# Polysketch attention and hash-routed experts on one core: q's features made with features on partitions

## Chip, core and metric

The kernel runs on one core of one Trainium2 chip. The metric is the time of one execution on the device in microseconds (us); lower is better. The time before is the median of three runs.

## The reference

```python
# q, k, v: (4, 4, 1088, 32) f32;  S1, S2: (8, 32) f64;  w1: (8, 128, 1024);  w2: (8, 1024, 128)
def phi(x):
    a = np.einsum('rd,bhsd->bhsr', S1, x)
    b = np.einsum('rd,bhsd->bhsr', S2, x)
    return np.einsum('bhsi,bhsj->bhsij', a, b).reshape(*x.shape[:-1], 64)
q_p, k_p = phi(q), phi(k)
kv = np.einsum('bhsf,bhsd->bhfd', k_p, v)
z = np.sum(k_p, axis=2)
num = np.einsum('bhsf,bhfd->bhsd', q_p, kv)
den = np.einsum('bhsf,bhf->bhs', q_p, z)[..., None] + 1e-06
x = (num / den).transpose(0, 2, 1, 3).reshape(4352, 128)

expert_idx = token_ids * 2654435761 % 8
for e in range(8):
    mask = expert_idx == e
    out[mask] = np.maximum(x[mask] @ w1[e], 0) @ w2[e]
```

Each row of q and k becomes 64 features, the products of 8 numbers from S1 with 8 numbers from S2. Everything after that is linear attention, and then one of eight experts for each token.

## The kernel before, in words

There are two stages: attention by batches (four of them, 0 to 3), and experts by groups of tokens. The order of the instructions of every engine is written out by hand: what stands in the source from top to bottom is what each engine gets, in its own queue and in that order. Tiles come from pools, and a pool with n buffers makes the n+1st tile wait until the first is read.

The attention of a batch of 1024 + 64 rows (the 64 are the "tail", kept in tiles of their own for all batches) goes so. `turned` and `turned_all` transpose k and q on TensorE, 128 rows by 128 columns at a time (four groups of 32 head columns), into one PSUM bank per half batch, and ScalarE copies them to `kT` and `qT`. `s_products` multiplies these as the stationary operand with `s_k`, the sketch laid out as a block diagonal of 128 rows by 64 columns. So the rows of the batch come out on partitions, and a and b of each of them lie along the free axis. ScalarE copies the a part (`first_copied`), and `features` multiplies a and b on VectorE to the 64 features of each row: `kp` for k, `f` for q, two instructions of 1024 columns each. `kv_products` accumulates kp against the values `va`, whose 33rd column of ones yields z. For q the 64 features must stand on partitions in the last product, so `q_turned` and `f_turned` transpose `f` again: 16 transposes a batch in four banks, each copied out to `fT` by ScalarE (by VectorE for every other one in the first and the last batch, `EVICT`). `x_products` multiplies fT with `m`, the kv product, in three PSUM tiles of at most three columns of rows each, ScalarE copies them to `xe`, `denominators` makes the reciprocals, and `x_main` (POOL, for batch 2 VectorE) and `x_rows` (DMA on SP's queue) write the rows to `x_rows` in DRAM.

The products of 64 columns run in two column halves of TensorE (`HALVES`, `tile_position=(0, 0)` or `(0, 64)`).

Between these stand, on VectorE and POOL above all, the steps that sort the tokens by expert (`route_...`). They end in `route_list`, 34 small matmuls, and `route_end`, which gives the index lists `get` and `put`.

In the expert stage `fetch_tile` gathers rows from DRAM by an indirect DMA on POOL's queue, `bring` and `bring_tile` transpose them on TensorE, `layer1` (L919) and `layer2` (L927) are the two products, `evict` takes layer 1 out of PSUM, and `scatter` writes the result. The last batch's x products stand in the first expert group, beside layer 1.

PSUM has eight banks: four in the pool `ps` (tag "b"), two in `ps_x` (tag "x") and two in `ps_o` (tag "o").

Of the kernel before, what the change touches and what calls it, by code (L numbers as in the profile page):

```python
# [30 lines left out]
def kernel(  # L31
# [12 lines left out]
    nc = tc.nc  # L44
# [37 lines left out]
    ps = ctx.enter_context(tc.tile_pool(name="ps", bufs=4, space=bass.MemoryType.PSUM))  # L82
    ps_x = ctx.enter_context(tc.tile_pool(name="ps_x", bufs=2, space=bass.MemoryType.PSUM))
    ps_o = ctx.enter_context(tc.tile_pool(name="ps_o", bufs=2, space=bass.MemoryType.PSUM))

    def bank(shape, name):
        return ps.tile(shape, F32, tag="b", name=name)

# [130 lines left out]
    def keep_busy(n, psum=None):  # L219

        if n == 0:
            return
        p = psum([P, 512], "idle") if psum else ps_o.tile([P, 512], F32, tag="o", name="idle")
        for _ in range(n):
            nc.tensor.matmul(p[:], warm[:].to_broadcast([P, P]), warm[:].to_broadcast([P, 512]), start=True, stop=True)

    keep_busy(WARM)
# [52 lines left out]
    s_k = const.tile([P, Q, 2, R], F32)  # L280

    def s_turned(psum):
        s_ps = psum([P, 2 * R], "s_ps")
        nc.tensor.transpose(s_ps[:], s_rep[:].rearrange("p t d -> p (t d)"), ident[:2 * R, :2 * R])
        nc.vector.tensor_tensor(s_k[:].rearrange("p t x r -> p t (x r)"), s_ps[:].unsqueeze(1).to_broadcast([P, Q, 2 * R]),
                                own_t[:].unsqueeze(2).to_broadcast([P, Q, 2 * R]), op=OP.mult)

# [32 lines left out]
    def route_counts():  # L320
        cnt = bank([P, 3, E], "cnt")
# [116 lines left out]
    def route_list():  # L438
        idx_ps = bank([P, 2, SE], "idx_ps")
# [23 lines left out]
    def x_bank(shape, name):  # L463
        return ps_x.tile(shape, F32, tag="x", name=name)

    def o_bank(shape, name):
        return ps_o.tile(shape, F32, tag="o", name=name)
# [4 lines left out]
    def turned(src, which):  # L472

        def half(g, heads=range(H)):
            p = bank([P, len(heads), P], "T_ps")
            for i, h in enumerate(heads):
                nc.tensor.transpose(p[:, i], src[:, h, g * Q:(g + 1) * Q].rearrange("p t d -> p (t d)"), ident[:])
            return p

        sT = work.tile([P, GQ, H, P], F32, tag=which, name=which, bufs=1)  # L480
        return sT, half

    def turned_all(src, which):
        sT, half = turned(src, which)
        for g in range(GQ):
            nc.scalar.copy(sT[:, g], half(g)[:])
        return sT
# [6 lines left out]
    def tail_products(sT):  # L494

        ab = bank([P, 2, TT, H, 2 * R], "abt_ps")
# [16 lines left out]
    def ab_bank(psum=o_bank):  # L513
        return psum([P, GQ, Q, H, 2 * R], "ab_ps")
# [58 lines left out]
    def f_turned(f, i):  # L573

        p = bank([P, 2, H // 2, P], "fT_ps")
        for t in range(2):
            for pr in range(H // 2):
                nc.tensor.transpose(p[:, t, pr], f[:, 2 * i + t, 2 * pr:2 * pr + 2].rearrange("p h i j -> p (h i j)"), ident[:])  # L578
        return p

    def q_turned(f, engs):

        fT = work.tile([P, T, H // 2, P], F32, tag="fT", name="fT", bufs=1)
        for i, eng in enumerate(engs):
            copy_of(eng)(fT[:, 2 * i:2 * i + 2], f_turned(f, i)[:])
        return fT

    def x_products(b, fT, m, psums=(x_bank, bank, x_bank)):

        for i, psum in enumerate(psums):  # L590
            lo = 3 * i
            n = min(3, T - lo)
            p = psum([P, n, H, DA], "x_ps")
            for t in range(n):
                for pr in range(H // 2):
                    for c, r in enumerate(HALVES):
                        nc.tensor.matmul(p[r, t, 2 * pr:2 * pr + 2].rearrange("p h d -> p (h d)"), fT[:, lo + t, pr, r],  # L597
# [4 lines left out]
    def x_tail_products(b, m, psum=x_bank):  # L602
# [113 lines left out]
    def bring(k, psum=x_bank):  # L716
# [32 lines left out]
    EVICT = (A, V, A, V)  # L749
    kT, _ = turned(k_t[0], "kT")  # L750

    def turned_head(src, sT, h):
        p = bank([P, GQ, P], "T_ps")
        for g in range(GQ):
            nc.tensor.transpose(p[:, g], src[:, h, g * Q:(g + 1) * Q].rearrange("p t d -> p (t d)"), ident[:])
        nc.scalar.copy(sT[:, :, h], p[:])

    for h in range(H):
        turned_head(k_t[0], kT, h)
        if h == 2:  # L760
            s_turned(x_bank)
    route_experts()
    ak, kp = first_of_ab(), feature_tile("kp")
    abk = [ab_bank(), ab_bank()]
# [5 lines left out]
    keep_busy(2, bank)  # L770
    qT, _ = turned(q_t[0], "qT")
    abq, aq, f = ab_bank(x_bank), first_of_ab(), feature_tile("f")
    for h in range(H + 1):
        if h < H:
            turned_head(q_t[0], qT, h)
        if h > 0:
            s_products(abq, qT, range(GQ), [h - 1])
    values(0, slice(0, H // 2), nc.scalar.copy)
    first_copied(aq, abq, range(GQ))
    values(0, slice(H // 2, H))  # L780
    kv = kv_products(0, kp, range(T), pairs=(0,))
    kv_products(0, kp, range(T), kv, (1,))
    nc.scalar.copy(cp[:], seq[:, :, C - 1])
    cnt = route_counts()
    features(f, aq, abq, range(GQ))
    route_places(cnt)
    route_order()
    kT = turned_all(k_t[1], "kT")
# [3 lines left out]
    def tail_f_turned():  # L792
        p = bank([P, TT, H // 2, P], "fTt_ps")
# [5 lines left out]
    for b in range(B - 1):  # L799
        last = b == B - 2  # L800
        if b > 1:
            kT = turned_all(k_t[b + 1], "kT")
        if b == 1:
            q_t.append(load_main(q, 3, "q", A.memzero))
        if last:
            qT = turned_all(q_t[b + 1], "qT")
        fT = q_turned(f, (A, A, A, A) if b > 0 else EVICT)
        if b == 0:
            route_bases(cnt)
            digits = route_ranks()  # L810
            tail_ps = bank([P, 2, TT, P], "tail_ps")
            tail_turned(k_tail, tail_ps, 0)
            tail_turned(q_tail, tail_ps, 1)
            tailT = work.tile([P, 2, TT, P], F32, tag="tailT", name="tailT", bufs=1)
            nc.scalar.copy(tailT[:], tail_ps[:])
            qT = turned_all(q_t[1], "qT")
            for u, va_tail in enumerate(va_tails):
                rows = tail_rows(u * TT)
                nc.gpsimd.tensor_copy(va_tail[rows, :, :, 0:D], v_tail[rows])
            tail_features(tail_products(tailT))  # L820
            route_parts(digits)
            route_order_end()
        elif not last:
            qT = turned_all(q_t[b + 1], "qT")
        if b == 1:
            v_t.append(load_main(v, 2, "v", A.memzero))
            route_in_tile()
        if last:
            idx = route_list()
            route_end(idx)  # L830
        if b > 0:
            kv = kv_products(b, kp, range(T + 1))
            m = kv_diagonal(b, kv)
        if b == 1:
            route_tiles_p()
        if last:
            load_expert(0, (2,), A.memzero)
        abq, aq, f = ab_bank(), first_of_ab(), feature_tile("f")
        s_products(abq, qT, range(GQ))
        first_copied(aq, abq, range(GQ))  # L840
        abk, ak, kp = ab_bank(), first_of_ab(), feature_tile("kp")
        s_products(abk, kT, range(GQ))
        first_copied(ak, abk, range(GQ))
        if b == 0:
            q_t.append(load_main(q, 2, "q", A.memzero))
            kT, half = turned(k_t[2], "kT")
            nc.scalar.copy(kT[:, 0], half(0)[:])
# [3 lines left out]
            nc.scalar.copy(kT[:, 1], half(1)[:])  # L851
        values(b + 1)
        if b == 1:
            v_t.append(load_main(v, 3, "v", A.memzero))
            load_expert(0, (1,))
            route_rows(0)
            route_tiles()
            route_rows(1)
            denominators(0)
            x_main_all(0)  # L860
            for g in range(GQ):
                x_rows(0, g)
            x_tail_rows(0)
        features(f, aq, abq, range(GQ))
        if b == 0:
            route_slots()
        x_products(b, fT, m)
        x_tail_products(b, m)
        if b == 0:
            k_t.append(load_main(k, 3, "k", A.memzero))  # L870
        if last:
            load_expert(1, (1,), A.memzero)
        if b == 0:
            features(kp, ak, abk, range(GQ))
        elif last:
            features(kp, ak, abk, range(GQ))
            denominators(b)
        else:
            denominators(b)
            features(kp, ak, abk, range(GQ))  # L880
        if 0 < b and not last:
            x_main_all(b)
        if b == 1:
            for g in range(GQ):
                x_rows(1, g)
            x_tail_rows(1)
        if last:
            for j in range(tiles_of(0)[1]):
                fetch_tile(0, j, True)

    e = B - 1
    fT = q_turned(f, EVICT)
# [4 lines left out]
    bring(0, o_bank)  # L897
    kv = kv_products(e, kp, range(T // 2, T + 1), kv)
# [6 lines left out]

    hots.release()
# [7 lines left out]
    def layer1(g, c, lo=0, hi=None):  # L914
# [3 lines left out]
        hp = bank([P, GL], "hp")  # L918
# [4 lines left out]
    def layer2(g, c, lo=0, hi=None):  # L923
        hi = hi or size_of(g)
        if c == 0:
            ops[g] = ps_o.tile([P, GL], F32, tag="o", name="op")
# [65 lines left out]
    def out_rows(i, n):  # L992
        tp = ps_x.tile([P, CT, P], F32, tag="x", name="tp")
# [51 lines left out]
    at(0, x3, x_products, e, fT, last_m)  # L1045
    at(0, x3, x_tail_products, e, last_m)
# [194 lines left out]
```

## Time and profile before

| | us |
|---|---|
| median of three runs | 180.3 (179.45 to 180.99) |
| profiled execution | 179.0 |
| its span | 177.2 |
| TensorE busy | 170.0 (96%) |
| VectorE busy | 95.8 (54%) |
| ScalarE busy | 67.7 (38%) |
| POOL busy | 93.4 (53%) |
| first matmul of layer 1 starts | 48.31 |

Engines in the profile: PE is TensorE's matmuls and PEld its weight loads, DVE is VectorE, ACT is ScalarE, POOL is GpSimd, SP issues most DMAs. The second part of the page cuts the span into 40 equal slices, 4.4 us each, and shows the busy share of each in tenths. In the timeline a line stands for a run of like instructions: its start, its length, the engine, the line of the source, the operation, output<-inputs, shape, and the number of records. TensorE is drawn as busy while a matmul is anywhere in its pipeline, so the starts tell more than the lengths.

### The profile page before, as it was taken

To read this page: it belongs to the slowest core of one execution; us is meant where nothing else is said; L and a number is where in the kernel's file an instruction comes from. 1 tells how busy PE (TensorE), PEld (TensorE's weight loads), DVE (VectorE), ACT (ScalarE), POOL (GpSimd) and SP (SyncE) were. 2 spreads that over 40 slices of the span, in tenths; PEclk is the share of its full clock that TensorE was granted. 3 is DMA by queue.
4 is the path that set the end of the run, shared out by engine and by line. 5 is a ranking of instruction groups with operands and counts; after the bars stand their busy time and mean duration, and the time that the engine had idled before them with its cause. 6 is when DMAs were issued, how large, how long until landed. Compare 5 with 4: busy or idle time off the path is not lost. (4 is left out here: it accounts for less than half of the span.)

```text
span 177.2 us, 4349 instructions
## 1 busy us (share of the span) xinstructions
PE 170.0 (96%) x1571; PEld 142.9 (81%) x1571; DVE 95.8 (54%) x309; ACT 67.7 (38%) x183; POOL 93.4 (53%) x134
## 2 busy tenths in 40 slices
PE   7899999999999999999999999999999999999980
PEld 3579899999886888888777778788788777778980
DVE  3688998996944333625535253535548543432330
ACT  3548686846452323133231422323232331320330
POOL 7313441774258366677756243773774760405752
PEclk9999999999999999999999999999999999999997
DMA  4897459485676869994983644484441522300100
GB/s 134 263 244 166 153 131 325 171 319 142 182 244 190 275 154 184 233 205 99 230 140 82 199 118 94 124 209 93 110 110 39 117 74 45 74 19 29 58 25 29
DMA packets 39382, 25.83 MB, mean 146 GB/s; under 512 B 20964, under 2 KB 35557, under 8 KB 39360
## 3 DMA queue, kind: packets, MB, share of 16 engines
q1 hardware_dynamic: 36944, 20.98, 45.4%
q0 software_dynamic: 2240, 4.53, 9.4%
q8 instruction: 13, 0.21, 0.5%
q14 instruction: 9, 0.07, 0.1%
q10 hardware_dynamic: 176, 0.04, 0.1%
HBM read 17.41 MB, written 4.52 MB: 124 GB/s over the span
## 5 line engine op out<-in xcount | busy, mean ns | idle before, releaser
L927 PE MATMUL op<-hT,w 128*128 128x256 f32 (+8 forms) x256 | 76.3, 389 | 0.0
L650 DVE TENSOR_SCALAR hT<-hp 128x256 f32<-128x256 f32 (+9 forms) x68 | 29.1, 428 | 59.1 <-PE hp L919 56.3
L927 PEld LDWEIGHTS op<-hT,w 128*128 128x128 f32 x256 | 47.5, 190 | 10.5
L930 POOL DMA_INDIRECT out_dram<-os,put x35 | 35.2, 1006 | 33.2 <-DVE os L988 16.3
L648 ACT ACTIVATE hT<-hp 128x256 f32<-128x256 f32 (+9 forms) x68 | 26.6, 391 | 63.2 <-PE hp L919 61.6
L642 POOL DMA_INDIRECT xg<-x_rows,idx x33 | 34.5, 1047 | 21.3 <-DVE idx L709 12.1
L919 PE MATMUL hp<-xT_late,w 128*128 128x320 f32 (+8 forms) x144 | 41.7, 385 | 0.0
L919 PE MATMUL hp<-xT,w 128*128 128x256 f32 x128 | 37.7, 381 | 0.0
L919 PEld LDWEIGHTS hp<-xT_late,w 128*128 128x128 f32 x144 | 25.3, 190 | 4.7
L919 PEld LDWEIGHTS hp<-xT,w 128*128 128x128 f32 x128 | 23.9, 191 | 5.5 <-ACT hT L648 0.4
L532 DVE TENSOR_TENSOR f<-first_of_ab,ab_ps 128x1024 f32<-128x1024 f32 x8 | 9.3, 1205 | 2.0 <-ACT first_of_ab L525 2.0
L532 DVE TENSOR_TENSOR kp<-first_of_ab,ab_ps 128x1024 f32<-128x1024 f32 x8 | 9.3, 1208 | 0.9 <-ACT first_of_ab L525 0.9
L561 PE MATMUL kv<-va,kp 128*64 128x33 f32 x256 | 8.4, 224 | 0.1
L561 PEld LDWEIGHTS kv<-va,kp 128*64 128x64 f32 x256 | 7.9, 138 | 0.8 <-issue 0.4
L597 PE MATMUL x_ps<-m,fT 128*64 128x66 f32 x256 | 8.3, 222 | 0.0
L552 POOL COPY va<-v 128x1024 f32<-128x1024 f32 (+1 forms) x4 | 3.7, 930 | 8.6 <-ACT v L117 4.3
L597 PEld LDWEIGHTS x_ps<-m,fT 128*64 128x64 f32 x256 | 7.8, 137 | 0.5 <-issue 0.5
L988 DVE COPY os<-turned 128x256 uint16<-128x256 uint16 (+1 forms) x26 | 7.3, 324 | 1.6 <-DMA xg<-x_rows,idx 1.0
L967 ACT COPY half<-op 128x256 uint16<-128x256 uint16 x16 | 5.2, 375 | 7.5 <-PE op L927 7.5
L578 PE MATMUL fT_ps<-ident,f 128*128 128x128 f32 x64 | 7.8, 274 | 0.0
L734 DVE COPY xh<-xg 128x256 uint16<-128x256 uint16 (+1 forms) x26 | 7.0, 313 | 1.2 <-DMA xg<-x_rows,idx 1.0
L578 PEld LDWEIGHTS fT_ps<-ident,f 128*128 128x128 f32 x64 | 7.0, 141 | 0.1
(199 smaller groups left out, 165.5 us busy)
## 6 DMA issues: line engine op xcount, KB each, us to landing
w<-in_moe_w_dram SPq DMA_DIRECT2D x20, 256.0 KB, 2.9
w<-in_moe_w_dram SPq DMA_DIRECT2D x6, 512.0 KB, 4.8
x_rows<-xs SPq DMA_DIRECT2D x8, 256.0 KB, 4.9
k<-in_k_dram SPq DMA_DIRECT2D x3, 512.0 KB, 6.8
q<-in_q_dram SPq DMA_DIRECT2D x3, 512.0 KB, 3.8
v<-in_v_dram SPq DMA_DIRECT2D x3, 512.0 KB
out_dram<-os,put POOLq DMA_INDIRECT x35, 2.5
xg<-x_rows,idx POOLq DMA_INDIRECT x33, 3.7
```

Of the source, the lines that this page charges most:

```text
L532: nc.vector.tensor_tensor(dst[:].rearrange("p t h i j -> p (t h) i j")[:, r], a[:, r].unsqueeze(3).to_broadcast(shape), rows_of_ab(ab)[:, ...
L561: nc.tensor.matmul(kv[h * R * R:(h + 1) * R * R, pr], f[:, 2 * pr + h].rearrange("p i j -> p (i j)"), v_[:, 2 * pr + h], start=(t == 0 and ...
L578: nc.tensor.transpose(p[:, t, pr], f[:, 2 * i + t, 2 * pr:2 * pr + 2].rearrange("p h i j -> p (h i j)"), ident[:])
L597: nc.tensor.matmul(p[r, t, 2 * pr:2 * pr + 2].rearrange("p h d -> p (h d)"), fT[:, lo + t, pr, r], m[:, pr].rearrange("p h d -> p (h d)"), ...
L642: nc.gpsimd.indirect_dma_start(out=dst, out_offset=None, in_=x_dram[0:rows], in_offset=bass.IndirectOffsetOnAxis(ap=idx, axis=0), bounds_c ...
L648: nc.scalar.activation(dst, src, AF.Relu if relu else AF.Copy)
L650: return nc.vector.tensor_scalar(dst, src, 0.0, None, op0=OP.max).ins
L734: nc.vector.tensor_copy(xh[:, x * w:(x + 1) * w], _half(xg3[k][:].rearrange("p a b -> p (a b)")[:, 0:w], x))
L919: nc.tensor.matmul(hp[:, 0:hi - lo], w1[:, g % E, c * P:(c + 1) * P], x_columns(first_of(g) + lo, first_of(g) + hi), start=True, stop=True)
L927: nc.tensor.matmul(ops[g][:, 0:hi - lo], w2[:, g % E, c], hTs[g][:, c, lo:hi], start=(c == 0), stop=(c == FC - 1))
L930: st_ = nc.gpsimd.indirect_dma_start(out=out[:], out_offset=bass.IndirectOffsetOnAxis(ap=idx, axis=0), in_=src, in_offset=None, bounds_che ...
L988: nc.vector.tensor_copy(_half(os[:].rearrange("p a b -> p (a b)"), x)[:, 0:n * DM], tts[x][:, 0:n].rearrange("p a b -> p (a b)"))
```

## The change

q's features are no longer made with rows on partitions and then transposed. Instead the sketch itself, each of its numbers repeated so that it has 64 columns for a and 64 for b (`s_q`), is the stationary operand, and `qT` is the moving one. The contraction is over the 32 columns of one head and one group of rows, so that a product takes 32 rows by 64 columns of TensorE, with 256 columns moving; `tile_position` names one of four row groups and one of two column halves. a and b come out with the 64 features on partitions; ScalarE copies a (`q_copied`), VectorE multiplies (`q_features`), and the result is `fT`. A batch is done in two pairs of heads, 16 products each. k's features are made as before.

```diff
+    one = ctx.enter_context(tc.tile_pool(name="one", bufs=1, space=bass.MemoryType.PSUM))
+    ps_q = tc.alloc_tile_pool(name="ps_q", bufs=2, space=bass.MemoryType.PSUM)
...
+    s_q = const.tile([P, 2, R, R], F32)
...
+        nc.vector.tensor_copy(s_q[:, 0], s_ps[:, 0:R].unsqueeze(2).to_broadcast([P, R, R]))
+        nc.vector.tensor_copy(s_q[:, 1], s_ps[:, R:2 * R].unsqueeze(1).to_broadcast([P, R, R]))
...
-    def f_turned(f, i):
-        p = bank([P, 2, H // 2, P], "fT_ps")
-        for t in range(2):
-            for pr in range(H // 2):
-                nc.tensor.transpose(p[:, t, pr], f[:, 2 * i + t, 2 * pr:2 * pr + 2].rearrange("p h i j -> p (h i j)"), ident[:])
-        return p
-    def q_turned(f, engs):
-        fT = work.tile([P, T, H // 2, P], F32, tag="fT", name="fT", bufs=1)
-        for i, eng in enumerate(engs):
-            copy_of(eng)(fT[:, 2 * i:2 * i + 2], f_turned(f, i)[:])
-        return fT
+    def q_products(qT, pr):
+        ab = [two_banks([P, 2, 2, GQ, P], "ab_q") for i in range(Q // 2)]
+        for c, cols in enumerate(HALVES):
+            for x in range(2):
+                for t in range(Q):
+                    rows = slice(t * D, (t + 1) * D)
+                    nc.tensor.matmul(ab[t // 2][cols, t % 2, x].rearrange("p g n -> p (g n)"),
+                                     s_q[rows, x].rearrange("p i j -> p (i j)"), qT[rows, :, 2 * pr + c],
+                                     start=True, stop=True, skip_group_check=True, tile_position=(rows.start, cols.start))
+        return ab
+    def q_copied(ab):
+        a = work.tile([P, 2, GQ, P], F32, tag="first_q", name="first_q", bufs=2)
+        nc.scalar.copy(a[:], ab[:, :, 0])
+        return a
+    def q_features(fT, pr, firsts, abs_):
+        fT[pr] = work.tile([P, GQ, Q, P], F32, tag="fT", name="fT", bufs=3)
+        for i, (a, ab) in enumerate(zip(firsts, abs_)):
+            nc.vector.tensor_tensor(fT[pr][:, :, 2 * i:2 * i + 2].rearrange("p g t n -> p t g n"), a[:], ab[:, :, 1], op=OP.mult)
```

In the attention stage PSUM is now two tiles of two banks each for q's products (`ps_q`, `two_banks`) and four single banks, each a tag of its own with one buffer: t and a (transposes, k's products) and x and y (kv, x products, tails). When the stage ends, `ps_q` is given up and the pool `ps` of four banks takes its place; the experts use t and a by turns where `ps_o` was, x and y by turns where `ps_x` was.

The order inside a batch is new. For batches 1 and 2 it reads (leaving out the steps of routing, the loads and the rows):

```python
kv = kv_products(b, kp, range(Q), own([P, H // 2, DA], "kv"))      # first half of the rows
k_half(1, t_bank if b == 1 else a_bank)()                          # k of the next batch
abq = q_products(qT, 1)
aq = [q_copied(ab) for ab in abq]
q_features(fT, 1, aq, abq)
s_products(abk, kT, range(GQ))
first_copied(ak, abk, range(GQ))
q_pair(0)()                                                        # q of the next batch
kv_products(b, kp, range(Q, T + 1), kv)
m = kv_diagonal(b, kv)
features(kp, ak, abk, range(GQ))
abq = q_products(qT, 0)                                            # of the next batch
aq = [q_copied(ab) for ab in abq]
q_features(next_fT, 0, aq, abq)
x_products(b, fT, m, range(2), (other, own))
q_pair(1)()
x_tail_products(b, m, other)
x_products(b, fT, m, range(2, 3), (0, 0, own))
denominators(b)
```

Routing moves with it: `route_list` of batch 2 stands behind q's second pair and k's products, and `route_slots` stands ahead of kp's first half in batch 0. In the last batch q's second pair stands between `bring(0)` and the second part of the kv products, just ahead of the experts.

## Prediction

> **What bounds the kernel now.** I read the page's busy table and slices first, then TensorE's waits, then the timeline of TensorE, and last the single start times of its matmul records, because a busy TensorE is not yet a full one.
>
> ```profile
> PE 170.0 (96%) x1571; PEld 142.9 (81%) x1571; DVE 95.8 (54%) x309; ACT 67.7 (38%) x183; POOL 93.4 (53%) x134
> PE   7899999999999999999999999999999999999980
> DVE  3688998996944333625535253535548543432330
> ```
>
> TensorE is the bound from about 10 us on. VectorE is close to it only in slices 3 to 11 (9 to 49 us), the attention stage that the change rewrites. The expert stage behind it (48 to 171 us) keeps its instructions, so what counts is by how much its first matmul, L919 at 48.31, moves.
>
> ```profile
> PE idle L225 <- POOL warm L180: 1.0, 1, 1.0
> PE s_ps L284 <- DVE s_rep L275: 0.4, 1, 0.4
> PE xp L726 <- DMA xg<-x_rows,idx: 0.3, 1, 0.3
> PE ab_ps L510 <- ACT qT L756: 0.2, 1, 0.2
> ```
>
> These are all of TensorE's waits: 1.9 us, none of them between 10 and 48 us. No eviction or feature product delays it there, so a shorter path on another engine gains nothing, and only TensorE's own work counts. One batch (b=1) in the timeline:
>
> ```profile
> 23.74 1.97 PE L578 MATMUL fT_ps<-ident,f 128*128 128x128 f32 x16
> 25.54 1.04 PE L477 MATMUL T_ps<-ident,q 128*128 128x128 f32 x8
> 26.51 2.06 PE L561 MATMUL kv<-va,kp 128*64 128x33 f32 x64
> 28.40 0.41 PE L561 MATMUL kv<-va_tail,f_tail 128*64 128x33 f32 x8
> 28.63 1.13 PE L510 MATMUL ab_ps<-s_k,qT 128*64 128x64 f32 x32
> 29.59 1.10 PE L510 MATMUL ab_ps<-s_k,kT 128*64 128x64 f32 x32
> 30.53 2.05 PE L597 MATMUL x_ps<-m,fT 128*64 128x66 f32 x64
> 32.40 0.40 PE L606 MATMUL x_ps<-m,fT_tail 128*64 128x66 f32 x4
> ```
>
> Columns: start, length, operation, records. Every matmul of this f32 data that is not a transpose leaves two records. The batch takes 8.99 us (23.74 to 32.73). Three prices come from the single starts. A transpose costs 109 ns. A 64-column record costs 29.2 ns where the two column halves alternate (L597, L510), but 58 ns where all sit on one half (L606): two halves really run at once. There the records start in pairs 7 ns apart from the very first, so a half is not held back by the other half's second record. Third, a change of tiling: the first 64-column record starts 203 ns after the last transpose (109 would be normal) and the second pair comes 20 to 48 ns late; back again it is 150 ns instead of 58, and the next gap 165 instead of 109. That is about 0.15 us for each change.
>
> **What the Trainium skill says.** TensorEngine Tiling (Array Packing), Key Properties: different tiles load and multiply in parallel, but changing the tiling mode drains the engine. The trace agrees with both (29 against 58 ns; 0.15 us). TensorE: Matmul & The Clock Gate, Part 3 (Measured speedup vs the span model): four row tiles of 32 gave 3.07 times, 16 row and column tiles 10.6 times, while matmuls start strictly in program order; the pairs 7 ns apart do not look like strict order if a matmul's two records stand together. No row tile is in the trace of before. TensorEngine Tiling, Gotcha 1: row tiles must write different PSUM banks; this is why the change needs two tiles of two banks.
>
> **The change, part by part.**
>
> Removed on TensorE: 64 transposes of f (L578), 64 x 109 = 7.0 us, and q's half of L510, 128 records x 29.2 = 3.7 us. Sum -10.7.
>
> Added: eight blocks (two per batch) of 16 products, 32 rows x 64 columns with 256 columns moving, 32 records a block. Nearest row: the 256-column f32 record of L919, 216 ns from start to start. Eight tiles exist, so each gets 4 records and 0.86 us is the floor. The loop runs all eight of the left half before the right half: if the right half can start only when the left one is half through, the block takes three steps of two records, 1.30 us. If only row groups overlap, 1.73; if each record waits for the one before on its tile and only the next tile's overlaps, 3.46; one by one 6.9. I take 1.1 because the 7 ns pairs show that a busy tile does not hold back the next one, at least one matmul deep. 8 x 1.1 = +8.8.
>
> Mode changes: in the order of instructions I count 24 of them on TensorE up to the first L919 and its x products before, and 41 after (q's blocks and the transposes now lie between the kv and x products): 17 x 0.15 = +2.5.
>
> TensorE's sum is -10.7 + 8.8 + 2.5 = +0.6 us.
>
> ACT and VectorE: q_copied (8 x 2 of 512 columns) replaces the 16 fT evictions at the same 0.5 us each (four of those were VectorE's, 0.69); four first copies of q (0.37) go. On VectorE four products of 512 columns a batch replace f's two of 1024: 4 x 0.65 (between half of 1.205 and the 0.682 of the 128x512 product, L623) against 2.3, +0.3 a batch. Both are covered by TensorE except where TensorE now waits for them. Two s_q copies at the start (about 0.15 each) stand behind s_k and ahead of nothing that is due before 6.9. DMA issues: the same loads, v's gate for batch 2 moved from ACT to POOL, one memset of about 0.1. SP's order is the same to within two places.
>
> Moved, with a wait: I laid the new order of each engine down with the durations above. (a) k's transposes of batch 1 start when the load lands at 12.4 instead of behind kv and the q work at 12.98: -0.5. (b) Batch 0: the third x chunk needs y's only bank, which ACT frees, about +0.5; then kv of batch 1 waits for kp's first half, because VectorE does route_slots before it (about 23.6), +0.2. (c) Batches 1 and 2: t's single bank is refilled after each eviction and the copy of batch 2's tiles (1.32 us on ACT, L436) stands ahead of kT's second half: +0.3 each. (d) bring(0). Before:
>
> ```profile
> 41.97 1.29 POOL L642 DMA_INDIRECT xg<-x_rows,get  x1 [2.82 <-issue]
> 46.66 0.44 PE L720 MATMUL xp<-ident,xg 128*128 128x128 f32 x2
> 48.31 1.13 PE L919 MATMUL hp<-xT,w 128*128 128x256 f32 x4
> ```
>
> The gathered rows landed at 46.34, just in time, and only 1.3 us of kv stood behind. Now q's last block stands behind too. The gather still waits for batch 1's rows to be stored (landed about 42) and for the index (about 42 now, since its 34 matmuls moved behind q's block), so it lands near 46.9, while TensorE arrives at about 46.1: +0.8. Queued behind are q's block (1.1), the kv products (1.3) and then L919. Sum of the waits: -0.5 + 0.7 + 0.6 + 0.8 = +1.6; some 0.5 us of the mode changes counted above lie inside these waits, so +1.1. L919 starts at 48.31 + 0.6 + 1.1 = 50.0.
>
> Given back: before, TensorE then waits for the second tile:
>
> ```profile
> 51.63 1.99 PE L919 MATMUL hp<-xT,w 128*128 128x256 f32 x8
> 53.92 0.33 PE L726 MATMUL xp<-ident,xg 128*128 128x128 f32 x1 [0.29 <-DMA xg<-x_rows,idx]
> ```
>
> Between 53.3 and 55 about 0.6 us are lost to this gather and the products that wait behind it. It is issued no later than before (its index copy no longer stands behind the fT evictions on VectorE), so a TensorE that is 1.7 us late does not wait. Net +1.1 us.
>
> The profiled execution took 179.0 us (span 177.2, 1.8 around it); the median shown is 180.3. 179.0 + 1.1 = 180.1 against itself, 180.3 + 1.1 = 181.4 against the median.
>
> **The rivals.** A difference below 1% (1.8 us) can hardly be told from none here.
> - Rows only (1.73 a block). For: no trace shows row and column tiles together, and the order gives all of the left half first. Against: the halves overlap fully in L597. The first block is hidden by the wait for k's load, so 7 x 0.63 = +4.4: 185.8.
> - Near-serial (3.46 a block): strict order of starts. Against: the 7 ns pairs. 7 x 2.36 = +16.5: 198.
> - Single banks: t, a, x and y have one bank each, where a pool of four turned before. If TensorE waits for one eviction (0.5) more in each of some six places: +3, 184.4. Against: ACT was 38% busy, and blocks of other banks stand between.
> - Other side, faster: the floor of 0.86 a block (7 x 0.24 = -1.7) and the 14 changes around q's blocks at half price (-1.0), with the gather early enough: -2.7 and 178.7. It decides only if bring(0) finds its rows by 45; with the wait still there 179.5.
> - That the change doesn't do what it says I exclude: the transposes and q's L510 are gone from TensorE's order.
>
> **How the numbers follow.** Forecast 181.4: 0.42, by itself 179.8 to 183. Rows only 0.20, near-serial 0.05, single banks 0.13, faster 0.20. Faster by over 1%: three quarters of the last, 0.15. Slower: 0.20 + 0.05 + 0.13 + a quarter of the forecast's, 0.49. Within 1%: 0.36. The range leaves out the near-serial case, the upper end of rows only together with the banks, and part of the faster case's tail: 178.3 to 187.5.
>
> **What would show it.** A block of q's 32 records lasts 1.0 to 1.3 us from its first start to the next operation's; more than 1.6 means rows only. Changes of mode cost 0.12 to 0.2. TensorE's waits name bring(0) (xp, gather) and kp's first half. L919 starts near 50.0, and the wait at the second tile is gone. If L919 starts before 48 or after 52, the sum is wrong; if it starts at 50 and the end moves by more than 2 us, something in the expert stage moved that I hold for unchanged.

## The result, and the profile after

| | before | after |
|---|---|---|
| median, 20 runs each (us) | 179.34 | 181.02 |
| ratio, 95% interval | | 1.009 [1.0063, 1.0117] |
| profiled execution, its span (us) | 179.0, 177.2 | 180.5, 178.8 |
| first matmul of layer 1 (us) | 48.31 | 50.51 |
| first matmul of layer 2 (us) | 55.89 | 57.41 |

The change costs 0.9%: a small loss, inside the 1% band of the forecast, though its interval reaches past that band and the forecast had given more chance to a loss of over 1% (0.49) than to one within it (0.36). The medians are of all 20 runs, the ratio leaves out those that ran in a slower state at a lower clock. The forecast of +1.1 us stands against +1.7 us between the medians and +1.5 us between the two profiled executions. The three runs shown at first had their median 1.0 us above that of the 20, so that 181.4 stands so near 181.02 by luck; the shift is what must be judged.

The page after, TensorE's and VectorE's busy time and slices, and the two groups of q's new path:

```profile
PE 169.6 (95%) x1635; PEld 138.3 (77%) x1635; DVE 93.2 (52%) x315; ACT 68.3 (38%) x182; POOL 95.3 (53%) x135
PE   7999989999699999999999999999999999999980
DVE  3777897988175335535345252634447553432330
...
L616 DVE TENSOR_TENSOR fT<-first_q,ab_q 128x512 f32<-128x512 f32 x16 | 10.2, 682 | 4.0 <-ACT first_q L609 4.0
...
L602 PE MATMUL ab_q<-qT,s_q 32*64 32x256 f32 x256 | 9.3, 387 | 0.0
```

TensorE is still the bound, with as much busy time as before and two dents that were not there: slice 6 (22 to 27 us) and slice 11 (45 to 49 us, a 6). Its waits name both:

```profile
PE xp L750 <- DMA xg<-x_rows,get: 1.2, 1, 1.2
PE idle L228 <- POOL warm L183: 1.0, 1, 1.0
PE kv L583 <- DVE kp L554: 0.6, 1, 0.6
PE T_ps L785 <- DMA k<-in_k_dram: 0.4, 1, 0.4
PE kv L583 <- POOL va L574: 0.4, 1, 0.4
PE x_ps L627 <- ACT xe L630: 0.3, 1, 0.3
PE kv L583 <- issue: 0.2, 1, 0.2
```

The columns are the total, the number of times and the longest. Before, TensorE had no wait of 0.2 us or more between 10 and 48 us. The last of these waits to fall stands ahead of q's last block, in the timeline of TensorE:

```profile
45.39 1.13 PE L583 MATMUL kv<-va,kp 128*64 128x33 f32 x32 [0.16 <-issue]
47.71 0.50 PE L750 MATMUL xp<-ident,xg 128*128 128x128 f32 x2 [1.19 <-DMA xg<-x_rows,get]
48.14 1.15 PE L602 MATMUL ab_q<-qT,s_q 32*64 32x256 f32 x32
49.22 1.12 PE L583 MATMUL kv<-va,kp 128*64 128x33 f32 x32
50.17 0.40 PE L583 MATMUL kv<-va_tail,f_tail 128*64 128x33 f32 x8
50.51 1.13 PE L974 MATMUL hp<-xT,w 128*128 128x256 f32 x4
...
55.66 0.27 PE L756 MATMUL xp<-ident,xg 128*128 128x128 f32 x1
...
57.41 0.59 PE L982 MATMUL op<-hT,w 128*128 128x256 f32 x2
```

The first layer 1 is 2.2 us later than before. The gathered tile at L756, for which TensorE waited 0.3 us before (L726 there), is there in time now, so the first layer 2 is only 1.52 us later; from there to the last layer 2 both kernels take 112.3 us. The loss is made before 57 us.

In the single starts, the 32 records of a block come in four waves of eight, in all blocks but the first. The eight of a wave start 6 to 7 ns apart (33 between the fourth and the fifth), and waves stand 216 ns apart, the first two 266. From the first start to 216 ns after the last one this is 0.99 us; from the first start to that of the next operation, with the change of mode, 1.08 us. The first block takes 1.22 us.

### The profile page after: what moved, and what is told of

Read it like the earlier page. It is cut to its first block, busy times and chain, and to the rows that moved or that the text cites. A ratio compares the mean times of both kernels' runs of the same rounds, so it can differ in the third digit from the quotient of the medians.

```text
span 178.8 us, 4493 instructions
## 1 busy us (share of the span) xinstructions
PE 169.6 (95%) x1635; PEld 138.3 (77%) x1635; DVE 93.2 (52%) x315; ACT 68.3 (38%) x182; POOL 95.3 (53%) x135
## 5 line engine op out<-in xcount | busy, mean ns | idle before, releaser
L616 DVE TENSOR_TENSOR fT<-first_q,ab_q 128x512 f32<-128x512 f32 x16 | 10.2, 682 | 4.0 <-ACT first_q L609 4.0
L653 POOL TENSOR_TENSOR xs<-xe,den 128x512 f32<-128x512 f32 x6 | 7.9, 1341 | 5.8 <-DVE den L647 5.7
L609 ACT COPY first_q<-ab_q 128x512 f32<-128x512 f32 x16 | 8.8, 589 | 4.6 <-PE ab_q L602 4.6
L583 PE MATMUL kv<-va,kp 128*64 128x33 f32 x256 | 9.0, 224 | 1.1 <-DVE kp L554 0.6
L627 PE MATMUL x_ps<-m,fT 128*64 128x66 f32 x256 | 9.2, 224 | 0.3 <-ACT xe L630 0.3
L602 PE MATMUL ab_q<-qT,s_q 32*64 32x256 f32 x256 | 9.3, 387 | 0.0
```

The lines of the kernel that those rows point to most:

```text
L583: nc.tensor.matmul(kv[h * R * R:(h + 1) * R * R, pr], f[:, 2 * pr + h].rearrange("p i j -> p (i j)"), v_[:, 2 * pr + h], start=(t == 0 and ...
L602: nc.tensor.matmul(ab[t // 2][cols, t % 2, x].rearrange("p g n -> p (g n)"), s_q[rows, x].rearrange("p i j -> p (i j)"), qT[rows, :, 2 * p ...
L609: nc.scalar.copy(a[:], ab[:, :, 0])
L616: nc.vector.tensor_tensor(fT[pr][:, :, 2 * i:2 * i + 2].rearrange("p g t n -> p t g n"), a[:], ab[:, :, 1], op=OP.mult)
```

## The experiments

All ratios are to the kernel before, run beside each kernel on the same chip. The runs form four sets, each on a chip of its own: `e0` to `e3`, `e4` to `e6`, `e7` to `e10`, and `e11`. Ratios of one set compare best.

**The changed kernel again** (`e0_after`, no edit), as a base for the first set: 1.0118 [1.0081, 1.0155].

> The changed kernel again, as the base of the three beside it. All theories: 0.9% slower than the kernel before (ratio 1.006 to 1.012), first layer-1 matmul near 50.5 us, one wait of 1.2 us at the first transposes of gathered rows.

**Do the row groups overlap?** (`e4_full_rows`) The sketch as a block diagonal, so that each product takes all 128 rows and only the column halves can overlap. The loop is turned too, so that the two halves alternate, and a tile of constants is made smaller to leave room.

```diff
-    s_q = const.tile([P, 2, R, R], F32)
+    s_q = const.tile([P, Q, 2, R, R], F32)      # zero off its own 32 rows
...
-        for c, cols in enumerate(HALVES):
+        for t in range(Q):
             for x in range(2):
-                for t in range(Q):
+                for c, cols in enumerate(HALVES):
...
-                                     s_q[rows, x]..., qT[rows, :, 2 * pr + c],
-                                     ..., tile_position=(rows.start, cols.start))
+                                     s_q[:, t, x]..., qT[:, :, 2 * pr + c],
+                                     ..., tile_position=(0, cols.start))
```

> q's products with all 128 rows: the sketch as a block diagonal with zeros, four row groups in one matmul's place, two column halves by turns; same number of matmuls, same output. Theory (in the changed kernel eight tiles run at once, 0.99 us for a block's 32 records): here two run at once, a block takes 32 x 216 / 2 = 3.46 us from first to last, 7 blocks on TensorE's path add 17 us, less some 1 us of changes of tiling; about 196 us. Rival (the row groups did not overlap, only the halves did): no change in a block, 181. Rival (rows overlap four at a time, halves not): the changed kernel's block would have been 1.73.

```profile
46.17 3.67 PE L602 MATMUL ab_q<-qT,s_q 128*64 128x256 f32 x32
49.67 1.10 PE L533 MATMUL ab_ps<-s_k,kT 128*64 128x64 f32 x32
```

A block takes 3.50 us to the next operation's start instead of 1.08, and the ratio is 1.0844 [1.0748, 1.0941], from two runs. The four row groups are worth a factor of 3.3 in a block.

**Does the order of the tiles matter?** (`e5_order`) The loop over row groups is made the outer one, so that the halves alternate.

```diff
-        for c, cols in enumerate(HALVES):
-            for x in range(2):
-                for t in range(Q):
+        for t in range(Q):
+            for x in range(2):
+                for c, cols in enumerate(HALVES):
```

> The loop of q's products turned: row group outermost, then a and b, then the column half, so that four matmuls of one row group stand together. Theory (each tile has a queue deep enough for two matmuls): a block still takes 0.99 us from its first to its last record's end, the same time. Rival (a tile holds one matmul that waits and then stops the ones behind it): the row groups start one after the other, some 0.43 us apart, 2.1 us a block, about +8 us. Rival (strict order of starts): 3.5 us a block.

```profile
41.94 1.16 PE L602 MATMUL ab_q<-qT,s_q 32*64 32x256 f32 x32
43.03 1.01 PE L627 MATMUL x_ps<-m,fT 128*64 128x66 f32 x22
```

The block is as long as before, 1.09 us. Here all products of one row group stand together ahead of the next group's, and neither a strict order of starts (3.5 us) nor a tile that can hold back only one matmul (2.1 us) would allow that. Its single time, 188.3 us beside a median of 185.3, settles nothing.

**The two waits, one at a time.** `e1_bring` moves the transposes of the gathered rows behind q's last block; `e2_slots` takes `route_slots` on VectorE from ahead of kp's first half in batch 0 to behind it.

```diff
-    bring(0, o_bank)
     abq = q_products(qT, 1)
     aq = [q_copied(ab) for ab in abq]
     q_features(fT, 1, aq, abq)
+    bring(0, o_bank)
```

> bring(0) moved behind q's last block. Theory (the end moves with the first layer-1 matmul, and the largest new wait ahead of it is bring(0) standing ahead of q's last block while the gathered rows land at 47.7): q's block (1.1 us with its changes of tiling) fills the wait, first layer-1 matmul at 49.3 to 49.5 instead of 50.5, the time 1.0 to 1.2 us less than the changed kernel's, about +0.3% against before. Rival (the gather's landing sets the end, whatever stands behind it): no change, 50.5. Rival (TensorE waits again at the second gathered tile): 49.4, but only 0.3 to 0.6 us come through to the end.

```diff
             route_order_end()
-            route_slots()
             kp = feature_tile("kp")
...
             features(kp, ak, abk, [0])
+            route_slots()
```

> route_slots moved behind kp's first half in batch 0. Theory: TensorE's 0.6 us wait for kp goes, the x products of batch 1 end 0.5 us earlier, but bring(0) still waits for a gather that is tied to the rows of batch 1: 0.3 to 0.6 us less than the changed kernel if the rows move with it, 0 if they don't. Rival (the slots' chain over POOL becomes late and holds in_tile and q's features): no change or 0.5 us slower.

`e1_bring`: 1.0086 [1.0052, 1.012]. From bring to the first layer 1 it is 1.72 us instead of 2.80, as expected. But bring itself came 0.9 us later: it stands behind the block now, this execution had lost 0.6 us before the last batch's first kv product (46.01 against 45.39), and the rows landed later too, so that 0.4 us of the wait is left. Counted from that product, layer 1 comes 0.8 us sooner (4.31 us behind it instead of 5.12). `e2_slots`: 1.0105 [1.0076, 1.0134]. The kp wait is gone and the first layer 1 stands at 49.50, 1.0 us earlier, 0.2 of which this execution was ahead by already at k's transposes of batch 1 (12.04 against 12.25); the wait for the rows remains. Neither can be told from the changed kernel (1.0118) by its time.

**Both at once** (`e7_two`):

> Both small moves at once: route_slots behind kp's first half in batch 0, and bring(0) behind q's last block. My theory (the two waits, 0.6 us for kp and 1.2 us for the gathered rows, are paid on TensorE's path and the end follows the first layer 1): kp's wait is gone, the gather is issued near 41.5 us and its rows land near 46.7 us, when TensorE is through with the block; L974 starts at 48.4 to 49.0 instead of 50.5, and the time is 1.2 to 1.8 us below the changed kernel's, that is within 0.5% of before. Rival A (the first expert group has slack of its own, so that an earlier L974 is lost again at its second gathered tile): L974 is as early, a wait of 0.5 us or more stands again at bring_tile L756, and the time falls by less than 0.8 us. Rival B (the gather always lands late): bring still waits 0.5 us or more and L974 is at 49.5 or later.

Its waits after the start, and its timeline:

```profile
PE x_ps L627 <- ACT xe L630: 0.3, 1, 0.3
PE kv L583 <- issue: 0.2, 1, 0.2
```

```profile
44.50 1.13 PE L583 MATMUL kv<-va,kp 128*64 128x33 f32 x32 [0.16 <-issue]
45.56 1.15 PE L602 MATMUL ab_q<-qT,s_q 32*64 32x256 f32 x32
46.63 0.49 PE L750 MATMUL xp<-ident,xg 128*128 128x128 f32 x2
...
48.34 1.13 PE L974 MATMUL hp<-xT,w 128*128 128x256 f32 x4
...
53.49 0.27 PE L756 MATMUL xp<-ident,xg 128*128 128x128 f32 x1
...
55.24 0.59 PE L982 MATMUL op<-hT,w 128*128 128x256 f32 x2
```

The ratio is 1.0017 [0.9983, 1.0051]: the loss is gone. Layer 1 begins at 48.34, where it began before the change, and no wait has come back at L756. So the loss was these two waits. Taking them away is worth 2.2 us at layer 1 (both executions reach k's transposes of batch 1 at 12.3): 0.9 up to the last batch's first kv product, the rest behind it. It is not a gain either: with the waits gone, TensorE's path is nearly as long as it was.

**What holds the gathered rows? First answer: their storing.** `e3_rows_dve` makes batch 1's rows on VectorE ahead of the routing, so that they are stored sooner.

```diff
             if b == 1:
+                for g in range(GQ):
+                    x_main(b, g, V)
+                    x_rows(1, g)
+                x_tail(b, V)
+                x_tail_rows(1)
                 route_tiles()
                 route_rows(1)
-            if b == 1:
-                x_main_all(b)
-                for g in range(GQ):
-                    x_rows(1, g)
-                x_tail_rows(1)
```

> Batch 1's rows are made on VectorE ahead of tiles and the second row table, instead of on POOL beside them (POOL took 3.5 us for the two products there, 2.1 at another place). Theory: the rows are stored 2 us earlier, the gather starts near 40.6 instead of 42.4 and lands by 46, bring(0) doesn't wait, first layer-1 matmul 1.1 to 1.3 us earlier, the time 1.0 to 1.3 us less. Rival (the index list, not the rows, holds the gather): gather not before 42, no change. Rival (VectorE gets late, the 34 index matmuls wait): bring's wait is traded for one at the index matmuls, 0 to +0.5 us.

Its ratio, 1.0141 [1.0103, 1.0179], is the largest of the set, but can't be told from the changed kernel's 1.0118. The gather, in the changed kernel and here:

```profile
42.38 1.29 POOL L672 DMA_INDIRECT xg<-x_rows,get  x1 [2.54 <-DVE kp L554]
```

```profile
42.85 1.29 POOL L672 DMA_INDIRECT xg<-x_rows,get  x1 [4.82 <-DVE get L464]
```

This execution was 0.9 us late before it reached the edit (35.23 against 34.32 at batch 2's first kv product), most of it lost at a load of v. Counted from there, the second half of the rows was sent off 2.3 us sooner (37.16 - 0.91 = 36.25 against 38.53), but the gather was issued only 0.4 us sooner (41.94 against 42.38), because the index list now stood behind that work on VectorE. TensorE waited 0.4 us in the index products and still 1.4 us for the rows, and layer 1, counted the same way, came 1.0 us later. `e6_all`, with this and both moves above, came to 1.0125 [1.0062, 1.0188]: the gain that the two moves bring was not seen. Why is not shown; in its one trace TensorE lost 1.9 us at the load of q's tail, at 17 us.

> The three moves together: bring(0) behind q's last block, route_slots behind kp's first half, batch 1's rows on VectorE. Theory: no wait of TensorE over 0.3 us between 12 and 50 us, first layer-1 matmul near 48.7 (50.5 less 1.2 for bring, less 0.6 for kp); the time 1.5 us less than the changed kernel's, within 0.3% of the kernel before. Rival (waits at the second gathered tile come back as TensorE gets earlier): 0.5 us of it lost.

**The same question with the storing taken out.** `e8_after_src` and `e9_before_src` let the first two gathers of the changed kernel and of the kernel before read rows of q, which need not be stored first. The results of the first expert group are then those of other rows.

```diff
+    q_rows = q.rearrange("b h (s c) d -> (b h s) (c d)", c=H)
...
-            out=dst, out_offset=None, in_=x_dram[0:rows],
+            out=dst, out_offset=None, in_=(x_dram if src is None else src)[0:rows],
...
-        gather(xg3[k][:, j], ..., NE if i + j < HT else N)
+        gather(xg3[k][:, j], ..., NE if i + j < HT else N, q_rows if k == 0 else None)
```

> The changed kernel, but the first expert group's two gathers read rows of q (the same number of bytes, by the same index list) in place of the attention's rows, so that they don't wait for these to be stored; the first group's results are therefore those of other rows. My theory: the gathers start when the index list is there (near 40.6 us), the rows land near 45 us, TensorE does not wait at bring, L974 starts at 49.3 us (1.2 earlier), and the time is about 1 us below the changed kernel's. Rival (the index list holds the gathers, as in the run with the rows made on VectorE): they start at 42 us or later and bring still waits for 0.8 us or more.

> The kernel before with the same replacement in its first two gathers. There bring never waited, so by every theory its first layer 1 stays at 48.3 us, give or take 0.2, and its time at that of before within 0.3%. The ratio of the run above to this one is then what the change costs without the wait for the gathered rows: by the measured terms 49.3 against 48.3, less some 0.7 us that the wait at the second tile gives back, +0.3 us or 0.2%; by the rival that a row-and-column block or a change of mode costs more than its starts show, +0.8 us or more.

`e9_before_src` behaves as expected: 0.9984 [0.9957, 1.0011], layer 1 at 48.10. `e8_after_src` does not: 1.0091 [1.0064, 1.0119], as slow as the changed kernel.

```profile
42.68 1.29 POOL L673 DMA_INDIRECT xg<-in_q_dram,get  x1 [0.87 <-DVE get L464]
```

```profile
47.36 1.13 PE L583 MATMUL kv<-va,kp 128*64 128x33 f32 x32 [0.16 <-issue]
48.42 0.33 PE L751 MATMUL xp<-ident,xg 128*128 128x128 f32 x1
49.64 0.33 PE L751 MATMUL xp<-ident,xg 128*128 128x128 f32 x1 [0.89 <-DMA xg<-in_q_dram,get]
...
52.26 1.13 PE L975 MATMUL hp<-xT,w 128*128 128x256 f32 x4
```

This execution is 1.97 us late as a whole at the first kv product of the last batch (47.36 against 45.39), 1.0 us of which it lost early, at a load of q's tail. Counted from that product, the gather was issued 1.67 us sooner than in the changed kernel (42.68 - 1.97 = 40.71 against 42.38), and the last of the rows landed no sooner (49.59 - 1.97 = 47.62 against about 47.6). Issuing it sooner is worth nothing here, so something else sets the landing. In each of the eight traces that show both, the rows land 5.6 to 6.4 us after one other transfer was issued, the 512 KB of expert 0's second weights (in the changed kernel L150, at 41.89). The two gathers of `e8_after_src` point to it as well: the first, issued 1.2 us ahead of this load (42.68 and 43.86), landed after 2.9 us, at 45.56; the second, issued 0.4 us behind it (44.27), took 5.3 us.

**Second answer: a weight load beside the gather** (`e11_weights`, on top of `e8_after_src`):

```diff
             if last:
-                load_expert(0, (2,), A.memzero)
                 route_end(idx)
...
+                load_expert(0, (2,), A.memzero)
                 load_expert(1, (1,), A.memzero)
                 for j in range(tiles_of(0)[1]):
                     fetch_tile(0, j, True)
```

The load's turn comes from ScalarE, which reaches it behind its x evictions now: it is issued at 46.64, 3.5 us after the second gather.

> The kernel with the first two gathers from q, and besides the 512 KB load of expert 0's second weights moved from ahead of these gathers to behind them (from 1.2 us after the first gather to some 3.5 us after it; it stands behind ScalarE's x evictions then). In all nine traces read so far the gathered rows landed 5.6 to 6.4 us after this load was issued, whether the gather itself was issued 4.4 or 7.2 us before that landing. My new theory (the gathers' rows share the DMA engines with this load and come in only when it is through): the second gather now lands within 4 us of its issue, bring does not wait, or less than 0.2 us, and L974 starts 0.9 to 1.2 us earlier counted from the first kv product of the last batch, that is within 3.9 us of it where the kernel with the load in its old place took 4.9 us; the time is 0.4 to 1.0 us below that kernel's. Rival (an indirect gather at this place takes 5 us or more whatever runs beside it): it lands 5 us or more after its issue and bring waits as before, 0.9 us.

```profile
43.11 0.99 POOL L673 DMA_INDIRECT xg<-in_q_dram,get  x1 [0.30 <-issue]
```

```profile
46.20 1.12 PE L583 MATMUL kv<-va,kp 128*64 128x33 f32 x32 [0.16 <-issue]
47.26 0.44 PE L751 MATMUL xp<-ident,xg 128*128 128x128 f32 x2
...
49.99 1.13 PE L975 MATMUL hp<-xT,w 128*128 128x256 f32 x4
```

The wait is gone: bring follows the kv product at once, within 4.2 us of the second gather's issue, and layer 1 comes 3.79 us after that kv product instead of 4.90. The ratio falls from 1.0091 to 1.004 [1.0012, 1.0068]; the two intervals touch, so it is the trace that carries the verdict. With q's rows as the source, the 512 KB load issued beside the gathers is what kept the last rows until 47.6.

The DMA packets that the traces keep show the same for the real source. A gather is 16 packets of 4 KB, the load 1024 of 512 bytes. In the changed kernel 30 of the two gathers' 32 packets start between 44.99 and 45.87, and the last two at 46.92 and 47.10, just behind the load's last at 46.89. In 11 of all 14 traces the gathers' last packet starts 0.03 to 0.22 us after the load's last one; in the kernel before, where the load was issued 1.5 us ahead of the first gather, it does not, nor in `e4_full_rows` and `e11_weights`.

Whether moving the load alone would have been enough with the real source was not tried, and probably it would not. From the second gather's issue to the end of its last packet it took 3.33 us in the changed kernel (43.97 to 47.30), 2.97 in `e11_weights` and 2.41 in the kernel before. An estimate from these three is that the load cost 0.4 to 0.9 of the 1.2 us; the rest would stay, with the gather issued at 42.38. The stored rows set that issue, since without them it came 1.67 us sooner.

**The changes of mode** (`e10_merge`, on top of `e8_after_src`): in batches 1 and 2, q's second transposes go behind all x products, which takes two changes of mode out of each.

```diff
-            q_pair(1)()
             x_tail_products(b, m, other)
             x_products(b, fT, m, range(2, 3), (0, 0, own))
+            q_pair(1)()
```

> The changed kernel with q's gathers as above, and in batches 1 and 2 the transposes of q's second pair moved from between the x products to behind them, next to k's transposes of the following batch where the routing allows it. That takes two changes of TensorE's mode out of each of the two batches. My theory (0.10 to 0.15 us for each): L974 0.4 to 0.6 us earlier than in the run with the gathers alone. Rival (the transposes covered the eviction of the x products: the third chunk's bank comes free late): a wait of 0.3 us or more for xe stands in each batch, and L974 does not move or moves back.

```profile
PE T_ps L494 <- ACT qT L508: 0.7, 1, 0.7
...
PE x_ps L627 <- ACT xe L630: 0.3, 1, 0.3
PE x_ps L636 <- ACT xe L630: 0.2, 1, 0.2
```

The rival was right in its outcome. The ratio, 1.0138 [1.0083, 1.0193], can't be told from the 1.0091 of `e8_after_src`, but in the trace layer 1 comes 1.4 us later, counted from batch 1's first kv product (27.71 us behind it instead of 26.29). The four transposes had filled the time in which ScalarE empties a bank. Ahead of the last batch, from q's block to the kv products, it takes 4.55 us (42.38 to 46.93) where it took 4.30, though two changes are gone; in the batch before, k's transposes now wait 0.7 us for ScalarE's copy of `qT`. The waits for xe that the rival had named are smaller than its 0.3 us in each batch.

## Why the prediction was right, and where its terms were off

- **The block, 1.1 us: a little high, by the right mechanism.** It measured 0.99 us. The forecast took one matmul's depth of queueing for each tile; the order of the loop turned out not to matter (`e5_order`), and all eight tiles run at once, near the floor of 0.86. Rows only (1.73) and near-serial (3.46) are refuted; `e4_full_rows` shows what the latter looks like, 3.50 us. The Trainium skill, TensorEngine Tiling (Array Packing), Key Properties, is borne out: tiles load and multiply side by side (32 records of 216 ns in 0.99 us). The strict order of starts that TensorE: Matmul & The Clock Gate, Part 3, states is not what these traces show: in the order of `e5_order` it would have made a block of 3.5 us, and 1.09 was measured. Its 3.07 times for four row tiles is close to the 3.3 here.
- **Changes of mode, 0.15 us each: right on the way in, a little high on the way out.** Into a q block the first start comes 203 ns after a transpose (109 is normal), and 50 ns more go at the block's first gap; out of it the next operation starts 305 ns after the last record (216 is normal), so 0.14 us in and at least 0.09 out. The count of 41 changes against 24 is what the traces have. What the forecast had no word for: a transpose between x products is also a cover for an eviction (`e10_merge`).
- **TensorE's own work, +0.6: near, somewhat high.** `e7_two` has no wait but 0.5 us in the attention stage. From k's transposes of batch 1 to layer 1 it takes 36.07 us (12.27 to 48.34), before 35.33 (12.98 to 48.31): +0.74 us with these 0.5, so about +0.3 by itself. The cheaper block (7 blocks in the path by 0.11) is part of that.
- **The waits, +1.6 gross: right in their sum, wrong in the terms.** The two that were the loss were put at 1.0 together and cost 2.2. The wait for kp's first half (b) was put at 0.2; it shows 0.6, and taking it away is worth 0.8 (`e2_slots`) to 0.9 (`e7_two`). bring's wait (d) was put at 0.8 and measured 1.2. The other terms were too high: earlier transposes of k (a) start at 12.25, -0.73 instead of -0.5, and of the 1.1 us for single banks (b, c) only 0.3 for xe shows, so that rival falls.
- **The reason for (d) was half of it.** The forecast let the gather be held by the stored rows and the index, and issued at about 42. That is so: it was issued at 42.38, and without the stored rows 1.7 us sooner. But its rows then landed no sooner, because the weight load beside it held the last of them, and the forecast had no term for that load. Its 0.8 us were too low by half for this. The first cure that followed from the reason given, storing the rows sooner (`e3_rows_dve`), brought nothing.
- **Given back, 0.6: right.** The wait at the second gathered tile is gone, and the first layer 2 is 0.7 us less late than the first layer 1.
- **The sum.** Layer 1 was put at 50.0, +1.7, and stood at 50.51, +2.2. By terms: the two waits +2.2 where the forecast had +1.0; the other waits with (a) -0.3 (0.3 and 0.2 of waiting less 0.7) where it had +0.6; TensorE's own work +0.3 where it had +0.1, because it took 0.5 of its 0.6 to lie inside the waits. Errors of +1.2 and -0.9 nearly cancel, so the nearness of +1.1 on the end to the measured +1.5 to +1.7 is in part luck; the mechanism, a path on TensorE of nearly the same length with new waits at kp and at bring, is not.
- **What stays open.** In four traces of edited kernels (`e6_all`, `e8_after_src`, `e10_merge`, `e11_weights`) TensorE waited 0.4 to 1.9 us between 15 and 17.5 us for the load of q's tail, and in neither trace of the old order. The changed kernel reaches these tails at 14.8 us, before at 15.6. That the new order runs against the loads there is likely, but no run took it apart.

## What to carry to other kernels

When TensorE is the bound and a change swaps its work one for one, look for the waits that its new order uncovers: here two of them, which show 0.6 and 1.2 us, were the whole loss, and two moved lines removed it. A transfer that lands late is not always issued late; see which large transfer was issued within a microsecond or two of it, and try moving that one. Before two traces are compared at a place, look whether one of them was late already: several executions here lost 0.7 to 1.9 us at earlier loads. Before two like operations are put together to save changes of mode, ask which eviction the operation between them was covering.

## What the runs showed of the hardware

- Eight f32 tiles of 32 rows by 64 columns run fully side by side: 32 records of 256 columns, at 216 ns each for one tile, took 0.99 us in all, and 3.50 us without the row groups. The order in which the tiles are named made next to no difference (1.09 against 1.08 us from the first start to the next operation's).
- Two 128-row gathers took 6.9 us from the first issue to the last landing beside a 512 KB load (42.68 to 49.59), and less than 5.8 us without it (41.52 to bring at 47.26), where the second was there within 4.2 us of its issue. In 11 of 14 traces the gathers' last packet started 0.03 to 0.22 us after the load's last.
- VectorE and POOL slowed each other. Where batch 1's rows (POOL, two products of 128x512) stood beside the routing's bf16 product on VectorE, POOL's two took 3.46 us instead of 2.06 before the change, and VectorE's product 2.13 us instead of the 1.28 of its other instances. In `e3_rows_dve`, where these rows are not on POOL, that same product took 1.28:

```profile
35.04 3.46 POOL L653 TENSOR_TENSOR xs<-xe,den 128x512 f32<-128x512 f32 x2 [4.46 <-DVE den L647]
35.46 2.13 DVE L425 TENSOR_TENSOR row<-number,st 128x2176 bf16<-128x2176 bf16 x1
```

```profile
38.80 1.28 DVE L425 TENSOR_TENSOR row<-number,st 128x2176 bf16<-128x2176 bf16 x1
```
